# Unit order on TensorE in the first batch of a fused attention and two-layer kernel, and the engine of some weight additions

## The chip, the cores and the metric

The kernel runs on one core of one Trainium2 chip. The metric is the device time of one execution in microseconds (us), the median of several runs. The engines are PE (TensorE), DVE (VectorE), ACT (ScalarE), POOL (GpSimd) and SP (SyncE, which here only issues DMAs).

## The reference

For 8 batches of 8 heads, 576 tokens and 64 features, a memory attention with 32 memory slots gives `x`; two feed-forward layers follow on the 4608 tokens of width 512:

```python
a = softmax(phi, over tokens)                  # 8 x 8 x 576 x 32
k_m, v_m = a^T k, a^T v                        # 8 x 8 x 32 x 64
x = softmax(q k_m^T / sqrt(64)) v_m            # -> 4608 x 512
x = (silu(x @ w_gate) * (x @ w_val)) @ w_out   # 512 -> 1536 -> 512
out = elu(x @ w_in) @ w_out2                   # 512 -> 2048 -> 512
```

The weights come as 64-bit floats. The kernel's matmuls run on pairs of 32-bit tiles, a high part and a low part, three matmuls for each product.

## The kernel before

**Weights.** `load_w` (L86) loads 128x512 doubles as pairs of 32-bit words (tile `wr`, 4 buffers) and turns them into fp32. For each piece ACT scales the upper words into `wv` (L100), DVE does four passes of 128x512 (L101 and L104, one tensor input; L102 and L105, two), and one or two last additions go to GpSimd. A gate piece (`load_wg`, tile `wg`) has one, L111. A split piece (`load_wo` for the first layer's output weights, `load_w2` for the second layer) is also rounded by ACT (L107) and has two, L108 and L109, that give `wlo`. `wv` and its partner `wc` have two buffers each, so the third piece waits until the first has had its last addition.

**First layer, first pass.** Heads are never brought back into token order for the gate. Instead `vw(b, p)` (L133) multiplies the value memory `vt` of batch b with gate piece p (8 matmuls `pvw`), and ACT (L143) and DVE (L144) split the result into high and low `vw`; `VW(b, 0)` serves units 0 and 1, `VW(b, 1)` units 2 and 3. The softmax weights `at` take the place of `x`. A unit u of a half batch (288 tokens) is `gate1` (six matmuls `pg`, then ACT tanh and DVE L176 make `s`) and `val1` (six matmuls `pv`, DVE L183 makes `h`, ACT L162 and DVE L164 split it to `hh` and `hl`). The four units of a half batch are followed, one half batch later, by `down1` (`pd`, 48 matmuls a half batch). `pg`, `pv`, `pd` and `pvw` share the three buffers of PSUM pool `ps_gv`.

**Attention.** `front_tasks(b)` transposes phi (`ps_aT`), multiplies it with k and v (`ps_kvm`, scaled by DVE L258 to `kvm`), and transposes the result (`ps_kvT`, copied to `kT` and `vt`). `back_tasks(b)` makes the scores (`ps_sc`, 8 matmuls for each half batch) and their softmax on DVE and ACT, up to `at` (L307, L308).

**Order.** The code before the batch loop does batch 0's attention, `vw(0, 0)`, four gate pieces for p = 1, and `vw(0, 1)` (L370). In the loop over b, `tick()` (L421) puts the tasks of the coming batches (`todo`) between the units of batch b; `done[0] + 3` over `spread` says how far it has come. For b = 0 `todo` starts with the four output weights alternating with batch 1's front. Tile's scheduler then orders each engine's queue; `issue_after` keeps what it covers behind a given instruction. Each engine runs its queue in order. The last gate and output pieces of this layer (p = 4 and 5, u = 4 to 11) are converted from batch 6 on; units 4 to 11 run in a second pass afterwards, and then the second layer.

Of the kernel before, what the change touches and what calls it, by code (L numbers as in the profile page):

```python
# [8 lines left out]
F32 = mybir.dt.float32  # L9
# [4 lines left out]
ALU = mybir.AluOpType  # L14
# [12 lines left out]
UA = 4  # L27
# [10 lines left out]
def attention_moe_moe(ctx: ExitStack, tc: tile.TileContext, qT, phiT, kv, kv4, w1g, w1o, w2, out):  # L38
    nc = tc.nc
    act = nc.scalar.activation  # L40
    tt = nc.vector.tensor_tensor
    stt = nc.vector.scalar_tensor_tensor
    mm = nc.tensor.matmul
    w1g, w1o, w2 = w1g.bitcast(I32), w1o.bitcast(I32), w2.bitcast(I32)
# [30 lines left out]
    last = {}  # L75
# [3 lines left out]
    def together(calls):  # L79
        first = calls[0]()  # L80
        with tc.issue_after(first.ins), tc.high_priority():
            for call in calls[1:]:
                call()


    def load_w(store, u, i, src, pool, split=True):  # L86
        raw = wr_p.tile([128, 512, 2], I32, tag="wr", name="wr")
        nc.sync.dma_start(out=raw, in_=src.rearrange("p (n t) -> p n t", t=2))
        lo32, hi32 = raw[:, :, 0], raw[:, :, 1]
        if split:  # L90
            hi = pool.tile([128, 512], F32R, tag="w", name="whi")
            lo = pool.tile([128, 512], F32R, tag="w", name="wlo")
        else:
            full = pool.tile([128, 512], F32, tag="w", name="wg")
        v = wt_p.tile([128, 512], F32, tag="wv", name="wv")
        c = wt_p.tile([128, 512], I32, tag="wc", name="wc")
        vi, cf = v.bitcast(I32), c.bitcast(F32)
        with tc.issue_after(last["h"].ins) if "h" in last else nullcontext():

            act(out=v, in_=hi32.bitcast(F32), func=AF.Copy, scale=2.0 ** -112)  # L100
            nc.vector.tensor_scalar(out=c, in0=vi, scalar1=3, scalar2=None, op0=ALU.logical_shift_left)  # L101
            stt(out=vi, in0=vi, scalar=-2 ** 31, in1=c, op0=ALU.bitwise_and, op1=ALU.bitwise_or)  # L102

            nc.vector.tensor_scalar(out=c, in0=vi, scalar1=-2 ** 23, scalar2=None, op0=ALU.bitwise_and)  # L104
            stt(out=cf, in0=lo32.bitcast(U32), scalar=2.0 ** -52, in1=cf, op0=ALU.mult, op1=ALU.mult)  # L105
            if split:
                act(out=hi, in_=v, func=AF.Copy)  # L107
                nc.gpsimd.tensor_tensor(out=v, in0=v, in1=hi.bitcast(F32), op=ALU.subtract)  # L108
                nc.gpsimd.tensor_tensor(out=lo, in0=v, in1=cf, op=ALU.add)  # L109
            else:  # L110
                nc.gpsimd.tensor_tensor(out=full, in0=v, in1=cf, op=ALU.add)  # L111
        store[u][i] = (hi, lo) if split else full


# [1 line left out]
    WO = [[None] for _ in range(NU1)]  # L116
# [3 lines left out]
        load_w(WG, p, k, w1g[p, k], pool, False)  # L120

    def load_wo(u, pool):
        load_w(WO, u, 0, w1o[u], pool)

    def load_w2(u, i, pool):
        load_w(W2, u, i, w2[u, :, i * 1024:(i + 1) * 1024], pool)
# [6 lines left out]
    def vw(b, p, pools):  # L133
        t = VW[b, p] = vx_p.tile([128, 2, 2, 512], F32R, tag="vx", name="vw")
        ps = [pool.tile([128, 512], F32, tag=tag, name="pvw") for pool, tag in pools]

        def head(j, g):
            r, c = slice(64 * g, 64 * g + 64), slice(32 * j, 32 * j + 32)
            return mm(ps[g][c], lhsT=Bs[b].vt[r, j, :], rhs=WG[p][j][r], start=True, stop=True)  # L139

        together([lambda j=j, g=g: head(j, g) for j in reversed(range(KD)) for g in (1, 0)])
        for g in range(2):
            act(out=t[:, 0, g, :], in_=ps[g], func=AF.Copy)  # L143
            tt(out=t[:, 1, g, :], in0=ps[g], in1=t[:, 0, g, :].bitcast(F32), op=ALU.subtract)  # L144

    def up1(ps, w, c0, at, s0):
        cs, ss = slice(c0, c0 + 128), slice(s0, s0 + HS)
        for g in range(2):
            wh, wl = w[:, 0, g, cs], w[:, 1, g, cs]
            ah, al = at[:, 0, g, ss], at[:, 1, g, ss]  # L150
            mm(ps, lhsT=wh, rhs=ah, start=g == 0, stop=False)  # L151
            mm(ps, lhsT=wh, rhs=al, start=False, stop=False)  # L152
            mm(ps, lhsT=wl, rhs=ah, start=False, stop=g == 1)  # L153

    def down(ps, w, hs, ms, start, stop):
        mm(ps, lhsT=w[0][:, ms], rhs=hs[0], start=start, stop=False)  # L156
# [181 lines left out]
    G2 = [(ps_gv, "g")] * 2  # L338
# [28 lines left out]
    for k in range(KD):  # L367
        load_wg(1, k, wa_p)
    load(Bs[1])
    vw(0, 1, G2)  # L370

    def down1(b, hf, hs, m):
        ps = ps_gv.tile([128, HS], F32, tag="g", name="pd")
# [18 lines left out]
    for b in range(B):  # L392
        todo = []
        bk = list(back_tasks(b + 1)) if b + 1 < B else []
        fr = list(front_tasks(b + 2)) if b + 2 < B else []
        if b == 0:
            wo = [lambda u=u: load_wo(u, wa_p) for u in range(UA)]
            f1 = [lambda: (Bs[1].phi(), load_q(Bs[1]))] + list(front_tasks(1)) + [lambda: Bs[2].phi()]
            for i in range(max(len(wo), len(f1))):
                todo += wo[i:i + 1] + f1[i:i + 1]  # L400
        if 1 <= b <= 4:
            bk += [lambda k=k, p=2 + (b - 1) // 2: load_wg(p, k, wa_p) for k in (0, 1) if b % 2] + \
                [lambda k=k, p=2 + (b - 1) // 2: load_wg(p, k, wa_p) for k in (2, 3) if b % 2 == 0]
        if b == B - 2:
            wb_p = ctx.enter_context(tc.tile_pool(name="wb", bufs=NWB))
            ps_vw = ctx.enter_context(tc.tile_pool(name="ps_vw", bufs=1, space=PSUM))
            V2 = [(ps_vw, "vw"), (ps_gv, "g")]
            fr += [lambda u=u: load_wo(u, wb_p) for u in (4, 5, 6)]
        if b == B - 1:
            fr.append(lambda: load2(0))  # L410
            fr += wg_tasks(4) + [lambda: load_wo(7, wb_p), lambda: vw(0, 2, V2), lambda: load_wo(8, wb_p)]
            fr += wg_tasks(5) + [lambda: load_wo(9, wb_p), lambda: vw(0, 3, V2), lambda: load_wo(10, wb_p),
                                 lambda: load_wo(11, wb_p)]
        for i in range(max(len(bk), len(fr))):
            todo += fr[i:i + 1] + bk[i:i + 1]
        if b + 1 < B:
            todo += vw_tasks(b + 1)
        done = [0, 0]
        spread = 18 if b == 0 else 16 if b < B - 2 else 24

        def tick():  # L421
            done[0] += 1
            upto = min(len(todo), -(-len(todo) * (done[0] + 3) // spread))
            while done[1] < upto:
                todo[done[1]]()
                done[1] += 1

        silu = b == B - 1
        tick()
        for hf in range(2):  # L430
            hs = []
            for u in range(UA):
                s = gate1(b, u, Bs[b].at, HS * hf, silu)
                tick()
                hs.append(val1(b, u, Bs[b].at, HS * hf, s, silu))
                tick()
                if prev:
                    down1(*prev, u)
                    tick()
            prev = b, hf, hs  # L440
        while done[1] < len(todo):
            tick()
        if b == B - 3:
            st_fr.close()
            st_ps.close()
# [179 lines left out]
```

## Time and profile before

| | |
|---|---|
| median of 3 runs | 1608.3 us (1608.15 to 1608.68) |
| profiled execution, its own time | 1609.4 us |
| its span | 1607.6 us |
| PE busy | 1533.4 us (95%) |
| DVE busy | 988.0 us (61%) |
| ACT busy | 654.0 us (41%) |
| POOL busy | 166.2 us (10%) |

The span runs from the first to the last instruction; 1.8 us of the profiled execution lie outside it. PE is busy almost everywhere but in the first 80 us, around 320 to 360 us, and around 800 to 900 us. Shares over the whole span hide this; the views below are read by stretch.

### The profile page before, as it was taken

To read this page: it belongs to the slowest core of one execution; us is meant where nothing else is said; L and a number is where in the kernel's file an instruction comes from. 1 tells how busy PE (TensorE), PEld (TensorE's weight loads), DVE (VectorE), ACT (ScalarE), POOL (GpSimd) and SP (SyncE) were. 2 spreads that over 40 slices of the span, in tenths; PEclk is the share of its full clock that TensorE was granted. 3 is DMA by queue.
4 is the path that set the end of the run, shared out by engine and by line. 5 is a ranking of instruction groups with operands and counts; after the bars stand their busy time and mean duration, and the time that the engine had idled before them with its cause. 6 is when DMAs were issued, how large, how long until landed. Compare 5 with 4: busy or idle time off the path is not lost.

```text
span 1607.6 us, 24193 instructions
## 1 busy us (share of the span) xinstructions
PE 1533.4 (95%) x9816; PEld 1311.5 (82%) x9816; DVE 988.0 (61%) x1702; ACT 654.0 (41%) x1249; POOL 166.2 (10%) x119
## 2 busy tenths in 40 slices
PE   3599999979999999999998999999999999999998
PEld 2478789769999999999976788888888888888887
DVE  7997876795444454435889755555555555555554
ACT  3455444543333333333544433334343434343333
POOL 1400010241101011000435100000000000000000
PEclk7799999999999999999999999999999999999999
DMA  8887332452322232211522101001010101010000
GB/s 346 293 307 265 109 112 75 170 192 72 106 77 82 73 102 86 73 60 45 157 85 74 53 1 45 9 6 48 1 53 0 53 0 53 1 53 1 27 1 27
DMA packets 62961, 136.32 MB, mean 85 GB/s; under 512 B 6528, under 2 KB 37248, under 8 KB 60800
## 3 DMA queue, kind: packets, MB, share of 16 engines
q1 hardware_dynamic: 53632, 125.32, 22.7%
q10 hardware_dynamic: 9216, 9.44, 1.7%
q8 instruction: 77, 1.26, 0.3%
q14 instruction: 36, 0.29, 0.1%
HBM read 96.99 MB, written 37.75 MB: 84 GB/s over the span
## 4 chain that ended last, share of the span: by engine, by line
PE 81%; DVE 14%; DMA 2%; issue 2%; ACT 1%; SPq 0%; POOL 0%; ACTq 0%; DVEq 0%; POOLq 0%
PE acc L565 7%; PE acc L564 7%; PE acc L566 7%; PE pu L538 7%; PE pu L539 7%; PE pu L540 7%; PE acc L156 4%; PE acc L157 4%; PE acc L158 4%; PE pg L151 3%; PE pv L151 3%; PE pv L153 3%; PE pg L153 3%; PE pv L152 3%; PE pg L152 3%; PE pvw L139 3%
## 5 line engine op out<-in xcount | busy, mean ns | idle before, releaser
L538 PE MATMUL pu<-x1s,whi 128*128 128x512 f32 x576 | 224.7, 390 | 2.5 <-DVE g L554 2.5
L564 PE MATMUL acc<-whi,hh 128*128 128x512 f32 x576 | 224.5, 390 | 2.1 <-ACT hh L162 2.1
L566 PE MATMUL acc<-whi,hl 128*128 128x512 f32 x576 | 222.4, 390 | 3.3 <-DVE hl L164 3.3
L540 PE MATMUL pu<-x1s,wlo 128*128 128x512 f32 x576 | 224.8, 390 | 0.0
L539 PE MATMUL pu<-x1s,whi 128*128 128x512 f32 x576 | 224.7, 390 | 0.0
L565 PE MATMUL acc<-wlo,hh 128*128 128x512 f32 x576 | 224.2, 389 | 0.0
L553 DVE SCALAR_TENSOR_TENSOR g<-e,g 128x512 f32<-128x512 f32 x144 | 107.5, 747 | 157.5 <-ACT g L552 157.5
L162 ACT ACTIVATE hh<-g 128x512 fp32r<-128x512 f32 x144 | 91.0, 632 | 216.9 <-DVE g L554 216.9
L551 ACT ACTIVATE e<-g 128x512 f32<-128x512 f32 x144 | 90.8, 631 | 210.0 <-DVE g L550 210.0
L183 DVE SCALAR_TENSOR_TENSOR h<-s,pv 128x288 f32<-128x288 f32 x192 | 86.5, 451 | 140.8 <-PE pv L153 118.6
L164 DVE TENSOR_TENSOR hl<-g,hh 128x512 fp32r<-128x512 f32 x144 | 99.9, 694 | 88.3 <-ACT hh L162 88.2
L156 PE MATMUL acc<-hh,whi 128*128 128x288 f32 x512 | 151.0, 296 | 0.0
L157 PE MATMUL acc<-hh,wlo 128*128 128x288 f32 x512 | 150.6, 294 | 0.0
L158 PE MATMUL acc<-hl,whi 128*128 128x288 f32 x512 | 149.4, 295 | 0.0
L162 ACT ACTIVATE hh<-h 128x288 fp32r<-128x288 f32 x192 | 85.1, 443 | 138.9 <-DVE h L183 137.2
L164 DVE TENSOR_TENSOR hl<-h,hh 128x288 fp32r<-128x288 f32 x192 | 97.0, 505 | 63.0 <-ACT hh L162 62.8
L550 DVE TENSOR_SCALAR g<-pu 128x512 f32<-128x512 f32 x144 | 99.1, 689 | 55.2 <-PE pu L540 51.8
L566 PEld LDWEIGHTS acc<-whi,hl 128*128 128x128 f32 x576 | 108.0, 188 | 28.4 <-DVE hl L164 6.1
L151 PE MATMUL pg<-at,vw 128*128 128x288 f32 x384 | 119.4, 311 | 10.4 <-DVE vw L144 6.0
L564 PEld LDWEIGHTS acc<-whi,hh 128*128 128x128 f32 x576 | 108.3, 188 | 25.4 <-ACT hh L162 3.0
L538 PEld LDWEIGHTS pu<-x1s,whi 128*128 128x128 f32 x576 | 108.3, 188 | 25.3 <-DVE g L554 2.9
L539 PEld LDWEIGHTS pu<-x1s,whi 128*128 128x128 f32 x576 | 108.5, 188 | 22.6
(87 smaller groups left out, 3187.9 us busy)
## 6 DMA issues: line engine op xcount, KB each, us to landing
kvr<-kv SPq DMA_DIRECT2D x32, 512.0 KB, 7.9
wr<-w SPq DMA_DIRECT2D x32, 512.0 KB, 3.6
wr<-w1g SPq DMA_DIRECT2D x24, 512.0 KB, 4.9
qr<-qT SPq DMA_DIRECT2D x16, 576.0 KB, 5.9
atd<-at SPq DMA_DIRECT2D x8, 1152.0 KB, 5.3
p1d<-p ACTq DMA_DIRECT2D x64, 144.0 KB, 2.0
p1l<-p1d SPq DMA_DIRECT2D x16, 576.0 KB, 4.1
at<-atd SPq DMA_DIRECT2D x8, 1152.0 KB, 5.2
```

The source lines that it names most:

```text
L151: mm(ps, lhsT=wh, rhs=ah, start=g == 0, stop=False)
L156: mm(ps, lhsT=w[0][:, ms], rhs=hs[0], start=start, stop=False)
L157: mm(ps, lhsT=w[1][:, ms], rhs=hs[0], start=False, stop=False)
L158: mm(ps, lhsT=w[0][:, ms], rhs=hs[1], start=False, stop=stop)
L162: act(out=hh, in_=h, func=AF.Copy)
L164: tt(out=hl, in0=h, in1=hh.bitcast(F32), op=ALU.subtract)
L538: mm(ps, lhsT=wh[:, k, :], rhs=xh, start=k == 0, stop=False)
L539: mm(ps, lhsT=wh[:, k, :], rhs=xl, start=False, stop=False)
L540: mm(ps, lhsT=wl[:, k, :], rhs=xh, start=False, stop=k == KD - 1)
L564: mm(accs[c], lhsT=hs[0][:, cs], rhs=wh, start=u == 0, stop=False)
L565: mm(accs[c], lhsT=hs[0][:, cs], rhs=wl_, start=False, stop=False)
L566: mm(accs[c], lhsT=hs[1][:, cs], rhs=wh, start=False, stop=u == NU2 - 1)
```

## The change

Three things are changed. `vw(0, 1)` is called after unit 1 of the first half batch, no longer ahead of the loop. For b = 0 `tick` starts four steps later (`- 1` for `+ 3`), and each task that it issues is put behind the last matmul that `up1` had issued by then. The last additions of all 24 gate pieces and of output pieces 0 to 3 go to DVE.

```diff
-    def load_w(store, u, i, src, pool, split=True):
+    def load_w(store, u, i, src, pool, split=True, own=False):
...
-                nc.gpsimd.tensor_tensor(out=v, in0=v, in1=hi.bitcast(F32), op=ALU.subtract)
-                nc.gpsimd.tensor_tensor(out=lo, in0=v, in1=cf, op=ALU.add)
+                part = tt if own else nc.gpsimd.tensor_tensor
+                part(out=v, in0=v, in1=hi.bitcast(F32), op=ALU.subtract)
+                part(out=lo, in0=v, in1=cf, op=ALU.add)
             else:
-                nc.gpsimd.tensor_tensor(out=full, in0=v, in1=cf, op=ALU.add)
+                tt(out=full, in0=v, in1=cf, op=ALU.add)
...
-        load_w(WO, u, 0, w1o[u], pool)
+        load_w(WO, u, 0, w1o[u], pool, own=u < UA)
...
-            mm(ps, lhsT=wl, rhs=ah, start=False, stop=g == 1)
+            last["pe"] = mm(ps, lhsT=wl, rhs=ah, start=False, stop=g == 1)
...
-    vw(0, 1, G2)
...
-            upto = min(len(todo), -(-len(todo) * (done[0] + 3) // spread))
+            upto = min(len(todo), -(-len(todo) * (done[0] + (3 if b else -1)) // spread))
             while done[1] < upto:
-                todo[done[1]]()
+                with nullcontext() if b else tc.issue_after(last["pe"].ins):
+                    todo[done[1]]()
                 done[1] += 1
...
+                if (b, hf, u) == (0, 0, 1):
+                    vw(0, 1, G2)
```

The changed file has one line more ahead of L108, so what was L139 is L140 in the rows of the change. This is PE's queue before, from `vw(0, 0)` to the first matmuls of batch 0's first unit; `ps_aT`, `ps_kvm`, `ps_kvT` and `ps_sc` are batch 1's attention, but the last `ps_aT` row, which is batch 2's:

```order
L139 MATMUL pvw<-wg,vt 32x512 x8
L235 MATMUL ps_aT<-ident,ph 128x128 x8
L229 MATMUL ps_aT<-ident,ph 128x128
L251 MATMUL ps_kvm<-kvr,a 32x128 x40
L265 MATMUL ps_kvT<-ident,kvm 128x128 x2
L280 MATMUL ps_sc<-qr,kT 32x288 x8
L235 MATMUL ps_aT<-ident,ph 128x128 x4
L139 MATMUL pvw<-wg,vt 32x512 x8
L151 MATMUL pg<-at,vw 128x288
```

And this is PE's queue in the change, from behind unit 1's `pg` to the first matmul of unit 2 (18 matmuls, `pg` and `pv` of unit 0 and `pg` of unit 1, stand between `vw(0, 0)` and the first row):

```order
L236 MATMUL ps_aT<-ident,ph 128x128 x4
L152 MATMUL pv<-at,vw 128x288
L153 MATMUL pv<-at,vw 128x288
L154 MATMUL pv<-at,vw 128x288
L152 MATMUL pv<-at,vw 128x288
L153 MATMUL pv<-at,vw 128x288
L154 MATMUL pv<-at,vw 128x288
L236 MATMUL ps_aT<-ident,ph 128x128 x4
L140 MATMUL pvw<-wg,vt 32x512 x8
L152 MATMUL pg<-at,vw 128x288
```

Units 0 and 1 of batch 0 now stand ahead of `vw(0, 1)`; of batch 1's front only the first eight transposes do. Its `ps_kvm` comes behind units 2 and 3, its `ps_kvT` and scores behind the first rows of `pd`.

DVE's queue before, in the conversions of the four gate pieces of p = 1:

```order
L101 TENSOR_SCALAR wc<-wv 128x512
L102 SCALAR_TENSOR_TENSOR wv<-wv,wc 128x512
L104 TENSOR_SCALAR wc<-wv 128x512
L105 SCALAR_TENSOR_TENSOR wc<-wr,wc 128x512
L101 TENSOR_SCALAR wc<-wv 128x512
L102 SCALAR_TENSOR_TENSOR wv<-wv,wc 128x512
L212 TENSOR_REDUCE nmx<-ph 128x2
L258 TENSOR_SCALAR kvm<-ps_kvm,rs 128x2x64 x2
```

The same place in the change:

```order
L105 SCALAR_TENSOR_TENSOR wc<-wr,wc 128x512
L184 SCALAR_TENSOR_TENSOR h<-s,pv 128x288
L105 SCALAR_TENSOR_TENSOR wc<-wr,wc 128x512
L177 SCALAR_TENSOR_TENSOR s<-s,pg 128x288
L112 TENSOR_TENSOR wg<-wv,wc 128x512
L165 TENSOR_TENSOR hl<-h,hh 128x288
L112 TENSOR_TENSOR wg<-wv,wc 128x512
L184 SCALAR_TENSOR_TENSOR h<-s,pv 128x288
```

The additions L112 stand in DVE's queue, and `s`, `h` and `hl` of units 0 and 1 among the conversions; `nmx` of batch 2 and `kvm` of batch 1 have moved behind all conversions of p = 1.

## Rows read from the trace of the kernel before

**Rows 1.** The page, part 1: busy time, share of the span, instructions.
```profile
PE 1533.4 (95%) x9816; PEld 1311.5 (82%) x9816; DVE 988.0 (61%) x1702; ACT 654.0 (41%) x1249; POOL 166.2 (10%) x119
```
**Rows 2.** Stretches of 40 us: length, busy us and instructions, PE clock, DMA share, GB/s.
```profile
0.00:40.00 40.00, 15.74 (x172) 7.87 (x176) 28.64 (x51) 15.13 (x29) 6.42 (x11) 0.73 0.89 347
40.00:80.00 40.00, 23.81 (x276) 16.66 (x269) 39.73 (x65) 17.39 (x38) 17.00 (x12) 0.76 0.80 290
...
400.00:440.00 40.00, 40.00 (x325) 37.00 (x324) 19.41 (x42) 15.22 (x33) 6.32 (x4) 1.00 0.35 119
```
**Rows 3.** Three chosen stretches, same columns (PE, PEld, DVE, ACT, POOL).
```profile
12.70:80.20 67.50, 35.27 (x402) 21.68 (x402) 66.88 (x112) 27.94 (x60) 22.79 (x16) 0.70 0.84 317
80.20:160.00 79.80, 77.89 (x912) 63.97 (x918) 69.77 (x153) 45.40 (x107) 2.56 (x2) 1.00 0.80 287
312.90:361.10 48.20, 39.21 (x304) 33.74 (x303) 46.57 (x71) 23.98 (x51) 21.25 (x15) 0.99 0.62 207
```
**Rows 4.** PE's waits from 28 to 100 us: total us, times, longest.
```profile
PE ps_kvT L265 <- DVE kvm L258: 7.1, 1, 7.1
PE ps_aT L235 <- ACT ph L215: 6.8, 3, 5.2
```
**Rows 5.** PE in order of time: start us, busy us, idle before and releaser.
```profile
50.07 0.69 PE L265 MATMUL ps_kvT<-ident,kvm 128*128 128x128 f32 x2 [7.06 <-DVE kvm L258]
...
55.50 0.61 PE L151 MATMUL pg<-at,vw 128*128 128x288 f32 x1
...
68.96 0.44 PE L153 MATMUL pg<-at,vw 128*128 128x288 f32 x1
69.20 0.44 PE L151 MATMUL pg<-at,vw 128*128 128x288 f32 x1
...
75.10 0.29 PE L151 MATMUL pg<-at,vw 128*128 128x288 f32 x1
75.23 0.29 PE L152 MATMUL pg<-at,vw 128*128 128x288 f32 x1
...
77.03 0.72 PE L280 MATMUL ps_sc<-qr,kT 64*32 64x288 f32 x16 [0.37 <-ACT kT L268]
...
80.73 0.30 PE L153 MATMUL pv<-at,vw 128*128 128x288 f32 x1
...
361.24 0.61 PE L151 MATMUL pg<-at,vw 128*128 128x288 f32 x1 [3.47 <-DVE vw L144]
```
**Rows 6.** DVE groups, 12.7 to 80.2 us: busy us, mean ns, idle before.
```profile
L102 DVE SCALAR_TENSOR_TENSOR wv<-wv,wc 128x512 int32<-128x512 int32 x12 | 11.9, 994 | 0.2
...
L164 DVE TENSOR_TENSOR hl<-h,hh 128x288 fp32r<-128x288 f32 x2 | 2.8, 1416 | 0.0
```
**Rows 7.** The same groups of DVE from 80.2 to 160 us.
```profile
L164 DVE TENSOR_TENSOR hl<-h,hh 128x288 fp32r<-128x288 f32 x16 | 7.2, 448 | 1.5 <-ACT hh L162 1.5
...
L102 DVE SCALAR_TENSOR_TENSOR wv<-wv,wc 128x512 int32<-128x512 int32 x3 | 2.0, 683 | 0.0
```
**Rows 8.** DVE in order of time, the last gate conversions of p = 1 and after.
```profile
50.27 0.41 DVE L101 TENSOR_SCALAR wc<-wv 128x512 int32<-128x512 int32 x1
50.61 0.68 DVE L105 SCALAR_TENSOR_TENSOR wc<-wr,wc 128x512 f32<-128x512 uint32 x1
51.21 0.68 DVE L102 SCALAR_TENSOR_TENSOR wv<-wv,wc 128x512 int32<-128x512 int32 x1
...
59.89 0.68 DVE L144 TENSOR_TENSOR vw<-pvw,vw 128x512 fp32r<-128x512 f32 x1
```
**Rows 9.** POOL in order of time, last gate addition of p = 1.
```profile
51.37 1.68 POOL L111 TENSOR_TENSOR wg<-wv,wc 128x512 f32<-128x512 f32 x1 [3.68 <-DVE wc L105]
```
**Rows 10.** The chain that ended last: start us, us, what; a batch's `ps_kvm`.
```profile
109.30 2.38 PE ps_kvm L251 x80
```
**Rows 11.** PE's waits from 280 to 400 us.
```profile
PE pg L151 <- DVE vw L144: 5.7, 2, 3.5
```
**Rows 12.** DMA issues up to 160 us: count, KB each, median us to landing.
```profile
ph<-phiT SPq DMA_DIRECT2D x8, 576.0 KB, 4.5
```

## Prediction

> **What bounds the kernel now.** I read the page first, then the span in stretches, then in each weak stretch PE's waits and the engine that they name. PE is busy 1533.4 us of the 1607.6 [rows 1], so no more than 74 us can be won without taking matmuls away, and the change takes none. The stretches say where these lie: PE is idle 24.3 us in the first 40 and 16.2 in the next 40, and not at all from 400 to 440 [rows 2]. From 12.7 to 80.2 us it is DVE that is full (66.9 of 67.5 us), with PE at 35.3 and a mean granted clock of 0.70; from 80.2 to 160 PE is full (77.9 of 79.8) and DVE has 10 us to spare; from 312.9 to 361.1 DVE is full again (46.6 of 48.2) and PE idles 9.0 [rows 3]. So the start is bound by DVE, then PE takes over, and around 340 DVE bounds once more.
>
> What PE waits for in the start is batch 1's attention: 7.1 us for `kvm` and 6.8 us for phi's softmax [rows 4]. Both stand in PE's queue ahead of batch 0's first unit, and `kvm` stands in DVE's queue among the conversions. The gap before `ps_kvT` at 50.07 is one piece of 7.06 us [rows 5]. After such a gap PE runs at the lower of its two levels (1.2 GHz): its 288-column matmuls start 0.24 us apart at 68.96, and 0.13 us apart at 75.10, at 2.4 GHz [rows 5].
>
> **The change: the additions.** Up to 80.2 us POOL does 16 additions, 22.8 us of its time [rows 3]. They cost DVE something too. L102 takes 994 ns in the mean of twelve there and 683 where POOL has next to nothing to do; L164 takes 1416 against 448 [rows 6, 7]. Read in this way, L102 and L164 lose 3.7 and 1.9 us; L101, L104, L105, L218, L289 and L298 lose 7.6 us more between them. Together that is 13.2 us, or 0.83 us for each addition on POOL. On DVE an addition is a pass with two tensor inputs like L105 or L102, which start 0.60 us apart at 50.61 and 51.21 [rows 8]; I take 0.61. So in the start DVE pays 16 x 0.61 = 9.8 and gets 13.2 back: 3.4 us.
>
> The Trainium skill (SBUF — State Buffer, Who interferes with whom) says that a DVE instruction with two SBUF inputs and a GpSimd instruction that reads SBUF exclude each other for a whole instruction, whichever starts first. The rows agree that there is a loss, at 0.83 us against the 1.42 us that a POOL addition lasts; with the whole 1.42 the start would give 22.8 - 9.8 = 13.0 us in place of 3.4.
>
> **The order.** Now when the pieces come. *Gate pieces of p = 1.* Before, DVE ends the last pass at 51.2 and POOL adds until 53.05 [rows 8, 9]. In the change the same point on DVE has 8 additions more (4.9 us) and six instructions of units 0 and 1 (`s`, `h`, `hl` at some 0.4 each, 2.3 us), less `nmx`, two `kvm` and an L101 that moved behind it (2.1 us), less what POOL took from DVE by then (eight additions at 0.83, 6.6 us): 51.2 + 4.9 + 2.3 - 2.1 - 6.6 = 49.7, some 3.4 us earlier. *`VW(0, 1)`.* From there thirteen DVE rows follow up to the second L144, nine of 0.60 and four of 0.34 us [rows 8]: 6.8 us, so 56.5, against 60.5 before (59.89 + 0.6). *Output pieces 0 to 3.* Another 10 us of such rows, with four of units: 66.5, against 80.1 before, because the scores of batches 1 and 2 no longer stand between them.
>
> PE starts batch 0's units at about 35, when `at` and `vw(0, 0)` are there, not at 55.5 [rows 5]. Units 0 and 1 and eight transposes at the lower clock last until 42; then PE waits for the gate pieces until 49.7, does `vw(0, 1)`, waits again until 56.5, and has units 2 and 3, batch 1's `ps_kvm` and unit 4 done at about 65.5. Before, PE has the same five units done at 80.9 [rows 5], and beside them batch 2's `ps_kvm` (2.4 us [rows 10]), three scores (0.7 each [rows 5]), ten transposes and two `ps_kvT` (some 1.9 together): 6.4 us of matmuls that the change still owes. So PE stands at 65.5 + 6.4 = 72 where it stood at 80.9: **9 us ahead**. From there it has the 96 matmuls of `down1` of batch 0 (12.8 us at 0.13) and three units, so it need not run dry before batch 1's `at`, which by the same count of rows comes at 79 and 85.
>
> Can that be kept? DVE is only 3.4 us ahead, and PE 9. In 80.2 to 160 us DVE has 10 us to spare [rows 3], so most of PE's lead can be followed. Against it: the batch of attention that stood ready before is not there, and PE takes its inputs in order. SP's queue has changed as well: batch 0's `at` store and the four output pieces go ahead of phi of batch 2, which can be fetched only when batch 1's ninth transpose is through (about 58), and lands 4.5 us later [rows 12], at 62.5; DVE wants it at about 63, with everything of the units queued behind. A slip there stops DVE for a microsecond. Between 3.4 (DVE's own gain) and 9 I take **7 us**.
>
> *The second DVE-bound stretch.* From 312.9 to 361.1 POOL has 15 additions, of which eight are gate pieces that move to DVE. They give back 8 x 0.83 = 6.6 us and cost 8 x 0.61 = 4.9: 1.7 us for DVE. PE waits there on DVE's `vw` (5.7 us in two waits [rows 11]) and the longer, 3.47 us, is followed by 18 matmuls at 0.24 us [rows 5], 2 us lost to the clock. If the gap shrinks enough, that returns too. Bounds: nothing, where output pieces on POOL still hold DVE, to 6 us; I take **2.5 us**. The eight gate pieces of p = 2 and 3, up to 240 us, fall where DVE has slack: nothing. From 400 us on PE is full [rows 2] and its queue hardly differs.
>
> Sum: 1609.4 - 7 - 2.5 = 1599.9 for an execution like the profiled one. The median is 1.1 us below that one, so **1598.8 us**.
>
> **Rivals.** *The additions alone count* (chance 0.14): PE's lead is eaten as it takes batch 1's and 2's attention in order behind DVE, and only DVE's 3.4 and 1.7 us remain: 1603.2. For it speaks that DVE is the full engine in both stretches; against it that PE's longest waits are for order, not for DVE's total. *The lead is lost altogether* (0.11): DVE halts for phi's landing, each halt leaves PE a gap, and each gap brings some 2 us at the lower clock; two or three such gaps and the 7 us are gone: 1607. *Slower* (0.10): before, batch 2's scores were done by 85 us, a batch ahead; without that reserve PE waits for `s`, `vw` or scores in each of batches 1 to 6. A wait of 1.5 us and the slower clock behind it, 3 us a batch, is 18 us against the 9.5 gained: 1617. It decides if the mean loss per batch exceeds 1.6 us. Against it stands DVE's slack of 10 us in 80. *The full lock* (0.05): each addition gives back 1.42 us, 13.0 us in the start and 11.4 - 4.9 = 6.5 later, 1588.8; the skill's page named above states that rule, the group means speak against it. That the change does not do what it says is out: the queues show both parts.
>
> **How the numbers follow.** The forecast of 1598.8 has 0.60, with 1593 to 1603 as its own range. About 0.2% (3.2 us) is what a measurement of this kernel can tell from no change. Faster by more than that, below 1605.1: 0.60 + 0.13 + 0.05, so 0.78; within it 0.13; slower 0.09. For eight in ten the range takes in the full lock and most of the case of a lost lead: 1589 to 1607.
>
> **What would show it.** In the profile of the change: no DVE row of L102 or L164 above 0.75 us before 80 us and no POOL addition before 280; the first `pg` before 37 us; the gate pieces of p = 1 done by 50 and `VW(0, 1)` by 57; batch 0's unit 4 by 66; PE idle from 28 to 81 us down from 23 to some 15 us, and two gaps of 4 to 7 us in place of the one before `ps_kvT`. From 80 to 280 PE's idle time should be no more than 3 us above before. The 48 us of the late stretch should shrink by 2 to 3. I am wrong if DVE shows idle time before 66 us (a DMA or ACT holds it), if PE's queue stops for `kvm` or `at` of batch 1, or if PE's waits grow in every batch up to 280 us.

## Result, and the profile after the change

| kernel | median of its runs, us | ratio to before, 95% interval |
|---|---|---|
| before | 1608.49 (1608.15 to 1611.86) | |
| changed | 1592.23 (1591.82 to 1594.32) | 0.9897 (0.988 to 0.9914) |

The change makes the kernel faster by 1.0%: 16.3 us between the medians, 17.6 between the two profiled executions (1609.4 and 1591.8 us). The forecast was 1598.8, a gain of 9.5, with a range from 1589 to 1607. So the sign and the range hold, and the gain was sized at somewhat more than half of what it is.

The page of the changed kernel, part 1 (busy time, share of the span, instructions), answers to [rows 1]:

```profile
PE 1526.8 (96%) x9816; PEld 1307.7 (82%) x9816; DVE 977.2 (61%) x1734; ACT 653.7 (41%) x1249; POOL 121.5 (8%) x87
```

The span went from 1607.6 to 1590.0 us. PE does the same 9816 matmuls; it is idle for 63.2 us in place of 74.2, which is 11.0 us, and busy for 6.6 us less. The second number is easily passed over: fewer busy microseconds for the same matmuls mean that PE spent less time at the lower of its two levels (the mean granted clock of the two executions is 0.981 before and 0.986 now).

The same stretches as in [rows 2, 3] (length, busy us and instructions of PE, PEld, DVE, ACT, POOL, then PE's clock, DMA share, GB/s):

```profile
0.00:40.00 40.00, 17.64 (x166) 11.32 (x167) 29.09 (x60) 15.13 (x30) 0.76 (x7) 0.74 0.92 363
40.00:80.00 40.00, 29.25 (x335) 22.73 (x338) 38.16 (x81) 21.30 (x47) 0.00 (x0) 0.79 0.74 249
...
80.20:160.00 79.80, 75.89 (x913) 59.45 (x904) 75.31 (x164) 44.22 (x104) 0.00 (x0) 1.00 0.89 315
312.90:361.10 48.20, 44.42 (x318) 38.22 (x317) 41.67 (x75) 25.29 (x54) 14.15 (x10) 0.93 0.52 176
```

PE does 5.4 us more in 40 to 80 us. The last row covers the same time as before and not the same work, which now stands 12 us earlier. The steps that took 48.2 us before take 42.8 now:

```profile
300.60:343.40 42.80, 39.70 (x310) 34.43 (x308) 39.49 (x76) 24.08 (x50) 7.68 (x6) 1.00 0.66 222
```

DVE has become a little less full there (92%, before 97%), and POOL does 6 additions beside it in place of 15. PE's waits from 28 to 81 us, total us, times and longest, answer to [rows 4]:

```profile
PE pvw L140 <- DVE wg L112: 12.3, 2, 7.3
PE pg L152 <- ACT at L308: 3.2, 1, 3.2
PE pg L152 <- ACT vw L144: 1.7, 1, 1.7
PE pg L154 <- DVE vw L145: 1.6, 1, 1.6
```

The waits for `kvm` and phi are gone from this stretch; PE waits for the gate pieces, as the order makes it. In order of time (start us, busy us, idle before and releaser) these are the first `pg`, `VW(0, 1)` and the end of unit 4:

```profile
32.79 0.61 PE L152 MATMUL pg<-at,vw 128*128 128x288 f32 x1 [3.20 <-ACT at L308]
...
48.11 1.11 PE L140 MATMUL pvw<-wg,vt 64*32 64x512 f32 x8 [7.30 <-DVE wg L112]
...
64.31 0.29 PE L154 MATMUL pv<-at,vw 128*128 128x288 f32 x1
```

And the DVE groups of 12.7 to 80.2 us (busy us, mean ns, idle before), which answer to [rows 6]:

```profile
L102 DVE SCALAR_TENSOR_TENSOR wv<-wv,wc 128x512 int32<-128x512 int32 x12 | 8.1, 684 | 0.1
...
L112 DVE TENSOR_TENSOR wg<-wv,wc 128x512 f32<-128x512 f32 x8 | 5.3, 677 | 0.0
...
L165 DVE TENSOR_TENSOR hl<-h,hh 128x288 fp32r<-128x288 f32 x7 | 3.1, 450 | 0.5 <-ACT hh L163 0.4
```

With POOL silent, L102 is at 684 ns (994 before) and L165 at 450 (1416).

**How far PE is ahead.** The tool for the rest is the lead: how much earlier than before a kernel starts the same step. Steps that both kernels have are the first matmuls of `VW(b, p)`, read from PE's rows in order of time. Behind 395 us the leads no longer move within the first layer. All numbers are us, from the profiled execution of each kernel; what was run is told below.

| kernel | VW(1, 0) | VW(3, 0) | VW(5, 0) | VW(7, 0) | behind 395 us |
|---|---|---|---|---|---|
| changed | 10.8 | 13.0 | 11.6 | 12.3 | 17.6 |
| order alone | 4.4 | -0.6 | -6.0 | -6.7 | -5.7 |
| additions alone | 5.9 | -2.6 | 0.4 | 0.2 | 6.3 |
| gate p = 0, 1 back on POOL | 3.6 | 1.5 | -1.4 | -0.6 | 4.3 |
| output 0 to 3 back on POOL | 8.4 | 6.4 | -0.4 | -0.7 | 4.4 |
| gate p = 2, 3 back on POOL | 10.3 | 12.2 | 3.7 | 3.0 | 10.2 |
| gate p = 4, 5 back on POOL | 9.8 | 11.1 | 9.8 | 10.5 | 11.0 |
| idle additions beside | 2.0 | 2.6 | -1.6 | -0.9 | 3.7 |
| only VW(0, 1) moved | -0.8 | -2.9 | 0.8 | -0.8 | 4.5 |
| order alone, PE filled | 4.2 | 3.8 | 0.2 | 0.3 | 0.9 |

The start gives 12.3 us, and the late stretch 5.3. Two limits go with these leads. Four of the kernels have the same queues on PE and DVE up to 260 us: the changed one, the one with gate p = 4, 5 given back, and the two told below that have all output additions, or all additions, on DVE. At VW(6, 0) their leads are 12.4, 10.5, 11.2 and 11.7, so a lead is good to some 2 us, and the 12.3 is from the highest of the four. And some profiled executions lie off their kernel's median: gate p = 0, 1 given back with 1605.4 us (median 1600.1), idle additions with 1605.7 (1602.3), all additions on DVE with 1577.0 (1581.4). The leads are read for where something is lost, the ratios below for how much. Up to batch 4 the columns are not quite the same amount of work, since the changed kernel owes some attention there. When every matmul is counted at its spacing at 2.4 GHz, the changed kernel has done at 71.4 us what before had done at 81.0: 9.6 us ahead.

### The profile page after: what moved, and what is told of

The parts are those of the page before. It is cut to its first block, busy times and chain, and to the rows that moved or that the text cites. A ratio compares the mean times of both kernels' runs of the same rounds, so it can differ in the third digit from the quotient of the medians.

```text
span 1590.0 us, 24178 instructions
## 1 busy us (share of the span) xinstructions
PE 1526.8 (96%) x9816; PEld 1307.7 (82%) x9816; DVE 977.2 (61%) x1734; ACT 653.7 (41%) x1249; POOL 121.5 (8%) x87
## 4 chain that ended last, share of the span: by engine, by line
PE 82%; DVE 13%; DMA 2%; issue 2%; ACT 1%; SPq 0%; ACTq 0%; DVEq 0%
PE acc L568 8%; PE acc L567 8%; PE acc L569 8%; PE pu L541 7%; PE pu L542 7%; PE pu L543 7%; PE acc L157 4%; PE acc L158 4%; PE acc L159 4%; PE pg L152 3%; PE pv L152 3%; PE pv L154 3%; PE pg L154 3%; PE pv L153 3%; PE pg L153 3%; PE pvw L140 2%
## 5 line engine op out<-in xcount | busy, mean ns | idle before, releaser
L165 DVE TENSOR_TENSOR hl<-g,hh 128x512 fp32r<-128x512 f32 x144 | 99.9, 694 | 87.7 <-ACT hh L163 87.6
L165 DVE TENSOR_TENSOR hl<-h,hh 128x288 fp32r<-128x288 f32 x192 | 89.4, 466 | 62.1 <-ACT hh L163 62.1
```

Source lines behind the costliest of these rows:

```text
L165: tt(out=hl, in0=h, in1=hh.bitcast(F32), op=ALU.subtract)
```

## The experiments

All were run with the kernel before beside them (medians 1609.7 to 1610.8 us), so ratios are compared; a difference in us is a difference of ratios times 1609 (by that count the change gives 16.6). One thing limits most of them: the scheduler orders the queues anew for every edit. Only the run with the idle additions has the queues of PE, DVE and ACT row by row as in the changed kernel, and the four kernels named above are alike up to 260 us. With the other edits some 40 to 180 of DVE's first 440 rows stand elsewhere, so each sizes its edit together with the order that came of it.

**The order alone, and the additions alone.** For the first, in the changed kernel:

```diff
-                tt(out=full, in0=v, in1=cf, op=ALU.add)
+                nc.gpsimd.tensor_tensor(out=full, in0=v, in1=cf, op=ALU.add)
...
-        load_w(WO, u, 0, w1o[u], pool, own=u < UA)
+        load_w(WO, u, 0, w1o[u], pool)
```

> The changed kernel with every addition of load_w given back to GpSimd: the order alone. Known: before 1608.5 us, changed 1592.2. Theory 1 (the parts add up): of the 12.3 us that PE leads by at batch 1 some 9 are the order's and 3.4 the additions', and the late stretch gives its 5 to the additions: 1608.5 - 9 = 1599.5 us, the first vw of batch 1 starting at about 78.5 us (75.7 in the changed kernel, 86.5 before). Theory 2 (the order carries the whole start): 1608.5 - 12.3 = 1596, vw of batch 1 by 76 to 77. Theory 3 (PE takes its inputs in order, so the order is worth little as long as DVE is slow): 1605 or more, vw of batch 1 after 83.

Measured: 1614.2 us, ratio 1.0024 (1.0014 to 1.0034). The order alone is slower than before, by 3.9 us. The third theory's bound (1605 or more) takes the time in, but no theory had a loss, and VW(1, 0) came at 82.1, ahead of the third's 83. The second is the kernel before with the lines of `load_w` and `load_wo` from the change, and its order as it was:

> The kernel before with the gate's additions and those of output pieces 0 to 3 on VectorE: the additions alone. Theory 1 (the parts add up): 3.4 us at the start and some 5 in the late stretch, 1608.5 - 8.4 = 1600 us, vw of batch 1 at 83. Theory 2 (only the late stretch is the additions'): 1603.5, vw of batch 1 at 86. Theory 3 (the additions carry the start, the order little): 1608.5 - 10 - 5 = 1594 to 1596, vw of batch 1 at 77 or before. As the prediction's rival had it: 1608.5 - 3.4 - 1.7 = 1603.4.

Measured: 1602.0 us, 0.9951 (0.9939 to 0.9963), 7.9 us faster. The total is the first theory's, but not its parts: the lead of 5.9 us at VW(1, 0) is gone at VW(3, 0), and 6 us come in the late stretch. So alone the two parts give +3.9 and -7.9, and together -16.6: most of the gain belongs to neither, it is there only with both. Where does the additions' early lead go? DVE and PE of that kernel in order of time:

```profile
79.84 0.56 DVE L259 TENSOR_SCALAR kvm<-ps_kvm,rs 128x128 f32<-128x128 f32 x2
81.86 1.35 DVE L213 TENSOR_REDUCE nmx<-ph 128x2 f32<-128x1152 f32 x1 [1.46 <-DMA ph<-phiT]
```
```profile
85.38 0.63 PE L140 MATMUL pvw<-wg,vt 64*32 64x512 f32 x4 [3.34 <-DVE s L177]
```

and its clock, in stretches:

```profile
80.00:86.00 6.00, 2.66 (x32) 1.23 (x34) 4.54 (x10) 3.52 (x10) 0.00 (x0) 1.00 1.02 387
86.00:92.80 6.80, 6.80 (x50) 4.09 (x36) 6.75 (x18) 2.62 (x5) 0.00 (x0) 0.50 0.89 358
```

DVE is early and finds phi not landed, with the DMA engines full (share 1.02 by the row); `s` is queued behind, PE stands for 3.34 us, and then runs 6.8 us at the lower clock. Up to 250 us DVE waits for phi 6.1 us in four waits; in the changed kernel it is 3.1 and before 2.5. The order alone loses in another place:

```profile
PE ps_kvT L266 <- DVE kvm L259: 2.9, 2, 1.5
```
```profile
115.30:129.00 13.70, 13.14 (x96) 7.32 (x99) 11.39 (x23) 5.93 (x12) 3.00 (x2) 0.50 0.87 308
```

PE's waits there are short (two for `kvm`, 2.9 us in all, from 80 to 240 us), but three stretches between 91 and 174 us, 23.9 us together, run at a clock of 0.50. At half the speed that is some 12 us lost, and the changed kernel has 1.00 from 60.2 to 240 (two of the kernels that share its queues there have one stretch of 3.4 us, at 106).

**Pieces given back one group at a time.** In the changed kernel, with `u` the number of the gate pair:

```diff
-                tt(out=full, in0=v, in1=cf, op=ALU.add)
+                (nc.gpsimd.tensor_tensor if u < 2 else tt)(out=full, in0=v, in1=cf, op=ALU.add)
```

and with `u in (2, 3)` or `u >= 4` for the other gate pairs; for output pieces 0 to 3, `own=u < UA` is left out.

> The changed kernel with the additions of the gate pieces p = 0 and 1 given back to GpSimd (8 of the 16 at the start), those of output pieces 0 to 3 on VectorE: the counterpart of the run with the output pieces given back (12 us slower). Theory 1 (each delay of VectorE at the start comes back enlarged, as PE runs into short waits up to 240 us and into the lower clock behind them): PE's VW(0, 1) starts 2 to 4 us later than at 48.1, the lead is down by 8 to 13 us at batch 5, 1592 + 10 = 1602. Rival (the parts add up; 22 us for all, less 6 for the late pieces, less 12 for the output pieces): 1592 + 4 = 1596.

> The changed kernel with the additions of output pieces 0 to 3 given back to GpSimd (8 of the 16 at the start, from 50 to 66 us); the gate's stay on VectorE. With all given back the changed order was 22 us slower than the changed kernel, 6 of which are the late stretch's. Theory 1 (each addition at the start counts alike): half of 16 us, so 1592 + 8 = 1600. Rival (the gate pieces of p = 1 decide, PE waits for them 10.3 us with GpSimd against 7.3): 1592 + 2. Rival (the output pieces decide, since down1 of the first half waits for them and PE's clock falls): 1592 + 13.

> The changed kernel with the additions of the gate pieces p = 2 and 3 given back to GpSimd (8 additions between 115 and 240 us). The prediction put them at nothing, since VectorE has slack there: 1592 within 1.5 us, the first vw of batches 1 and 2 at 75.7 and 101.4 as in the changed kernel. Rival (they stretch VectorE's rows just where PE has short waits for it, in 120 to 160 us VectorE is busy 38.8 of 40): 3 to 6 us slower, with PE's waits between 120 and 240 us longer or a stretch at the lower clock there that the changed kernel has not.

> The changed kernel with the eight additions of the gate pieces p = 4 and 5 (the late stretch) given back to GpSimd, all else as changed: it sizes the late stretch. Theory 1 (those eight make the 5 us that the lead grows by between 290 and 380 us): 1592.2 + 5 = 1597 us, the lead over before constant at about 12.3 us from there on. As predicted (2.5 us, the rest comes from elsewhere): 1594.7. Rival (nothing: the seven output additions that stay on GpSimd hold VectorE anyway, and the gap closes because PE arrives earlier): 1592.2.

| given back to POOL | ratio | 95% interval | us slower than changed |
|---|---|---|---|
| gate p = 0, 1 | 0.9940 | 0.9924 to 0.9955 | 6.9 |
| output 0 to 3 | 0.9972 | 0.9961 to 0.9982 | 12.1 |
| gate p = 2, 3 | 0.9933 | 0.9921 to 0.9945 | 5.8 |
| gate p = 4, 5 | 0.9936 | 0.9922 to 0.9951 | 6.3 |

Each group of eight costs 6 to 12 us. They add up to 31 us, but all of them given back cost 20.4 (1.0024 against 0.9897): a lead can be lost once only. The third theory held for the output pieces; for the gate pieces p = 0 and 1 the interval lies between the two theories. The late pieces are 6.3 us, and their lead stays at 10.5 to 11.0 behind 250 us where the changed kernel's grows: here the first theory holds, not the prediction's 2.5.

The pieces p = 2 and 3, which the prediction put at nothing, have their own lesson. From VW(3, 0) to VW(4, 0) the lead falls from 12.2 to 2.8, in the changed kernel from 13.0 to 9.2. Between them stands this, on DVE:

```profile
156.26 0.76 DVE L299 TENSOR_TENSOR sc<-sc,smx 128x576 f32<-128x576 f32 x1
159.78 1.35 DVE L213 TENSOR_REDUCE nmx<-ph 128x2 f32<-128x1152 f32 x1 [2.76 <-DMA ph<-phiT]
161.05 0.60 DVE L259 TENSOR_SCALAR kvm<-ps_kvm,rs 128x128 f32<-128x128 f32 x2
```

`kvm` stands behind `nmx` here and ahead of it in the changed kernel, phi lands 2 us later, PE waits 2.9 us for `kvm`, and from 161.3 to 168.1 its clock is 0.50. POOL's two additions at 149 and 151 us stretch L105 from 0.64 to 0.97 us and L290 from 0.74 to 0.85 beside them: the additions' own price is below 0.5 us, and what comes of it in this execution is 5.6. The 5.8 us of the runs agrees; why phi lands later is not shown, and as `kvm` has changed places, the order that came of the edit is a part of the price.

**Of the order, the one moved step.** The changed kernel with `done[0] + 3` for every batch and without the hold behind the last matmul:

```diff
-            upto = min(len(todo), -(-len(todo) * (done[0] + (3 if b else -1)) // spread))
+            upto = min(len(todo), -(-len(todo) * (done[0] + 3) // spread))
...
-                with nullcontext() if b else tc.issue_after(last["pe"].ins):
-                    todo[done[1]]()
+                todo[done[1]]()
```

> The changed kernel without its two rules on the tasks of batch 0 (three ticks ahead as before, and not held behind the last value matmul): of the order only VW(0, 1) is still moved behind unit 1. Theory 1 (the attention of batches 1 and 2 then stands on VectorE and PE ahead of output pieces and units again, and half of the start's gain of order goes): 1592.2 + 4 to 5 = 1597 us. Rival (the one moved step lets units 0 and 1 run early, and that is all of it): 1592 to 1593. Rival (the rules do it all, the early units only fill what was idle): 1601, the first vw of batch 1 at 84.

Measured: 1603.2 us, 0.9956 (0.9942 to 0.997), 9.5 us slower than the changed kernel, and VW(1, 0) at 87.3. In time that is the last rival (0.9956 of 1608.5 is 1601.4; VW(1, 0) is 3 us later than it said): with the additions on DVE but without the two rules, nothing is left of the start's gain, and the time is that of the additions alone. So the rules are needed. Whether they would do it all without the moved step was not run.

**What POOL takes from DVE.** Does an addition on POOL cost by what waits for it, or by what it does to DVE? The changed kernel, with 16 additions on POOL that write a tile which nobody reads:

```diff
-                part(out=lo, in0=v, in1=cf, op=ALU.add)
+                part(out=lo, in0=v, in1=cf, op=ALU.add); own and [beside(hi, lo) for _ in range(2)]
...
-                tt(out=full, in0=v, in1=cf, op=ALU.add)
+                tt(out=full, in0=v, in1=cf, op=ALU.add); u < 2 and beside(full, full)
...
+    beside = lambda x, y: nc.gpsimd.tensor_tensor(out=idle_t, in0=x.bitcast(F32), in1=y.bitcast(F32), op=ALU.add)
```

> The changed kernel, and beside it GpSimd does 16 additions that nothing waits for: as many and as large as before, each reading a piece that VectorE has just finished (p = 0 and 1 of the gate, output pieces 0 to 3). It tells what GpSimd takes from VectorE apart from the wait for GpSimd's result. Theory 1 (the loss is in VectorE's instructions beside GpSimd's): 16 x 0.83 = 13 us more on VectorE before 80 us, L102 near 0.99 us there, the first vw of batch 1 10 us later (at 86) and most of the changed kernel's lead gone: 1592 + 10 or more = 1602 to 1606. Rival (the loss was the chain through GpSimd, 1.4 us behind each piece and two buffers held): VectorE's rows as in the changed kernel and the time within 2 us of it.

Measured: 1602.3 us, 0.9954 (0.994 to 0.9969): 9.2 us slower than the changed kernel, VW(1, 0) at 84.6. As nothing else in the queues differs and no engine waits for POOL, this is shown to be what POOL's additions do to DVE. The first theory holds in time, but the rows that pay are others. DVE's groups from 12.7 to 70 us, in the changed kernel and then with the idle additions:

```profile
L102 DVE SCALAR_TENSOR_TENSOR wv<-wv,wc 128x512 int32<-128x512 int32 x12 | 8.1, 684 | 0.1
...
L101 DVE TENSOR_SCALAR wc<-wv 128x512 int32<-128x512 int32 x12 | 5.0, 418 | 4.5 <-ACT wv L100 4.4
L104 DVE TENSOR_SCALAR wc<-wv 128x512 int32<-128x512 int32 x12 | 4.9, 417 | 0.1
```
```profile
L102 DVE SCALAR_TENSOR_TENSOR wv<-wv,wc 128x512 int32<-128x512 int32 x12 | 8.8, 742 | 0.1
...
L101 DVE TENSOR_SCALAR wc<-wv 128x512 int32<-128x512 int32 x12 | 8.4, 706 | 4.5 <-ACT wv L100 4.4
L104 DVE TENSOR_SCALAR wc<-wv 128x512 int32<-128x512 int32 x12 | 6.4, 543 | 0.1
```

An addition that starts when DVE ends a piece meets the next piece's L101 and L104, not L102. L101, L102, L104, L105 and L110 lose 7.5 us together up to 70 us, where POOL has not yet done all of its 16 additions. Counted row by row up to 80 us DVE loses 9.7 us, or 0.6 for each addition. In the order alone, where POOL adds where it did before, L102 is at 1185 ns and L165 at 1173 (up to 70 us):

```profile
L102 DVE SCALAR_TENSOR_TENSOR wv<-wv,wc 128x512 int32<-128x512 int32 x12 | 14.2, 1185 | 0.2
...
L165 DVE TENSOR_TENSOR hl<-h,hh 128x288 fp32r<-128x288 f32 x3 | 3.5, 1173 | 0.0
```

The same count of L101 to L105, L165 and L290 makes 12.9 us, or 0.81 for each of 16: the prediction's 0.83.

**The clock by itself.** The order alone, and twelve transposes that nobody reads behind the matmuls of `ps_kvm` in batches 2 and 3:

```diff
+            for _ in range(12 if self.b in (2, 3) else 0):
+                with tc.issue_after(last["pe"].ins): nc.tensor.transpose(out=fill, in_=ident, identity=ident)
```

> The order alone (1614 us, 22 above the changed kernel), and in batches 2 and 3 twelve transposes of the identity, which nobody reads, behind the matmuls of ps_kvm: 1.4 us of work each time, as long as PE's two waits for kvm that stand there just ahead of the stretches at the lower clock from 91.4 to 94.8 and from 115.3 to 129.0 us. Theory 1 (of what the order alone loses between 80 and 205 us, two thirds or more is the lower clock behind those waits, so work in their place costs nothing and keeps the clock): neither stretch is there, 1614 - 6 to - 8.5 = 1606 to 1608. Rival (it is the waits themselves and those behind them that cost): 1614 within 2. Rival (the transposes are only work more): 1614 + 2.8 = 1617.

Measured: 1610.1 us, 0.9994 (0.9985 to 1.0004), against 1.0024 (1.0014 to 1.0034) without them: PE was given 24 matmuls more and the kernel became 4.8 us faster. In the profiled executions the lead behind 395 us goes from -5.7 to 0.9. The stretches in order:

```profile
80.00:119.50 39.50, 35.90 (x459) 26.33 (x462) 37.31 (x78) 21.81 (x51) 3.41 (x2) 1.00 0.82 277
119.50:122.90 3.40, 3.40 (x30) 1.91 (x19) 3.40 (x8) 2.29 (x4) 0.00 (x0) 0.50 0.94 358
122.90:198.00 75.10, 73.61 (x866) 63.66 (x872) 63.64 (x140) 37.80 (x93) 2.54 (x2) 1.00 0.67 238
```

Of 23.9 us at 0.50 between 80 and 200 us 3.4 are left. So the direction is the first theory's and the size a little short of it, and some 5 of the 20 us between the order alone and the change go with PE's short waits and the clock behind them. That it is the clock alone is not shown, since PE's queue differs in more than the transposes: at 95 us the scores now stand ahead of a unit's `pg`, in the order alone behind it. How the rest divides is argued from the traces, not shown.

**All additions on DVE.** `own=True` for every output piece, and then `part = tt` for every piece, the second layer's too:

> The changed kernel with the additions of output pieces 4 to 11 on VectorE as well (16 additions between 160 and 360 us, the last ones beside PE's gaps of 0.9, 1.8 and 0.7 us and a stretch of 6.8 us at the lower clock around 343). Theory 1 (an addition on GpSimd takes more of VectorE than it costs there, 0.83 against 0.61 us, and delays what waits for it): the gaps and that stretch go, 3 to 6 us, a ratio to the changed kernel of 0.996 to 0.998. Rival (the late stretch is no longer bound by VectorE, whose share there is 33.5 of 40 us): no change. Rival (16 more passes, 9.8 us, in VectorE's queue ahead of the units): 2 to 4 us slower.

> The changed kernel with every addition of load_w on VectorE, the 64 of the second layer's pieces too. Theory 1 (as for the output pieces): these 64 give VectorE back some 64 x 0.2 = 14 us in the stretch from 720 to 880 us, where PE idles 7.5 us in gaps of 2.5 to 0.9; half of that goes, 4 us beside those of the output pieces. Rival (the 64 additions of 0.61 us, 39 us, stand in VectorE's queue between a unit's g and its hl, so the gaps before acc grow): 3 to 10 us slower than with the output pieces alone.

Measured: 1588.1 us, 0.9869 (0.9854 to 0.9883), and 1581.4 us, 0.983 (0.9815 to 0.9845). Both are the first theory in time, the second with more than it forecast; the stretch at the lower clock around 343 us is halved (3.4 us left) with the output pieces alone and gone with all. The second kernel beats both kernels of this case, by 1.7% and 0.7%. From 800 to 880 us, in the changed kernel and with all on DVE, and DVE's costliest group there from 780:

```profile
800.00:880.00 80.00, 71.38 (x302) 55.81 (x303) 77.74 (x107) 38.49 (x63) 40.59 (x26) 1.00 0.18 60
```
```profile
L556 DVE SCALAR_TENSOR_TENSOR g<-e,g 128x512 f32<-128x512 f32 x14 | 17.5, 1255 | 2.6 <-ACT g L555 2.6
```
```profile
800.00:880.00 80.00, 79.37 (x350) 65.40 (x349) 75.69 (x136) 43.75 (x71) 0.00 (x0) 1.00 0.17 60
```
```profile
L556 DVE SCALAR_TENSOR_TENSOR g<-e,g 128x512 f32<-128x512 f32 x18 | 12.5, 705 | 3.2 <-ACT g L555 3.2
```

DVE does 136 instructions where it did 107, in less time, and PE's idle time there falls from 8.6 us to 0.6. Part of that is the window, since the same steps come 6 to 15 us earlier: from 720 to 960 us PE's idle time falls from 9.2 us to 3.4.

**Filling PE's wait at the start.** The kernel with all additions on DVE, and 36 transposes ahead of VW(0, 1):

```diff
+        for _ in range(36 if (b, p) == (0, 1) else 0):
+            nc.tensor.transpose(out=ps[0][:, 0:128], in_=ident, identity=ident)
```

> The kernel with all additions on VectorE (0.983 of before, 1581 us), and 36 transposes of the identity ahead of VW(0, 1), where PE waits 6.9 us for the last gate piece, up to 48.1 us. Theory 1 (the start up to 55 us is bound by VectorE, and from there PE runs units 2 and 3 at the lower clock up to 60.9 only because it had waited): PE is at 2.4 GHz by 48, units 2 and 3 and batch 1's ps_kvm are done 2 to 3 us earlier, and that is kept, 1581.4 - 2.5 = 1579. Rival (the two waits of 1.7 us for vw that follow bring the clock down again): 1581 within 1. Rival (PE arrives earlier and waits for VectorE later): 1581 within 1, with the first vw of batch 1 at 74 and that of batch 5 at 219 as without.

Measured: 1582.9 us, 0.9824 (0.9809 to 0.9839) against 0.983: no difference. The transposes end at 44.2 us, VW(0, 1) still waits 3.93 us, and the clock, at 1.00 up to there, falls again:

```profile
40.12 4.09 PE L143 MATMUL pvw<-ident 128*128 128x128 f32 x36
48.14 1.75 PE L140 MATMUL pvw<-wg,vt 64*32 64x512 f32 x16 [3.93 <-DVE wg L112]
```
```profile
38.20:48.50 10.30, 6.37 (x60) 5.77 (x66) 10.10 (x22) 4.78 (x9) 0.00 (x0) 1.00 0.67 238
48.50:58.70 10.20, 7.74 (x55) 4.98 (x43) 10.17 (x22) 5.56 (x12) 0.00 (x0) 0.50 0.62 195
```

In time that fits the first rival, but not its reason: the clock is at 0.50 from 48.5 us on, behind what is left of the wait for `wg` and ahead of the first wait for `vw`, which ends at 51.06. The gate pieces are ready at 48.1 us with the transposes and without, so DVE sets the time there. PE's `ps_kvm` does come 2.6 us earlier (57.9 in place of 60.5), as the first theory had it, but the gain is not kept: VW(1, 0) starts at 77.1 us, and at 76.2 without the transposes. As the queues behind differ too, what takes it is open.

## Why the prediction came out as it did

**The dates at the start were right.** Forecast and found: first `pg` before 37 (32.8), gate pieces p = 1 by 49.7 (48.0, where L112 ends), the last `vw` of VW(0, 1) by 56.5 (55.1), output pieces 0 to 3 by 66.5 (65.0), unit 4 by 65.5 (64.6). PE's idle time from 28 to 81 us was to fall from 23 to some 15: it is 14.3. The lead was counted as 9 at before's 80.9 us; by equal work it is 9.6. No addition ran on POOL there. Of the other signs two missed: POOL's first addition came at 272 us, not behind 280, and the late stretch shrank by 5.3 us, not by 2 to 3. One reading was off: the matmuls at 68.96 us [rows 5] were not slow because of the gap that ended at 50.07, since the clock was at 1.00 from 56.2 to 66.4 us in between; the gap they follow is a later one.

**The discount failed.** From 9 the prediction took 7, since DVE was only 3.4 us ahead and phi might halt it. In fact the lead went up, to 12.3 (10.5 to 12.4 in the four executions named above). PE's idle time from 80 to 240 us is 7.7 us against 7.1 before, as was foreseen. What differs is a stretch at the lower clock that only the kernel before has; in order of time, its PE row ahead of that stretch, and the stretch:

```profile
197.84 0.40 PE L151 MATMUL pv<-at,vw 128*128 128x288 f32 x1 [1.49 <-DVE s L176]
```
```profile
199.50:206.40 6.90, 6.90 (x32) 5.04 (x29) 4.99 (x8) 3.18 (x7) 2.55 (x2) 0.51 0.52 161
```

By equal work the lead goes from 8.8 us ahead of this stretch to 11.6 behind it. For this pair of executions that closes the account: 9.6 us, 2.7 more by 300 us, which is about what this stretch gives, and 5.3 in the late stretch are the 17.6 us. Some of it may be luck: one trace of the kernel before is kept, 2.7 us is near the scatter of the leads, and whether its other executions have the stretch is not shown. For it speaks that three kernels whose lead is gone have one at the same place (from 200 to 207 us with the output pieces given back and with the idle additions, from 203.7 to 207.1 with gate p = 0, 1). The clock stood in the prediction only as a price of the change's own gaps; that the kernel before had such a stretch to lose was in the trace and was not looked for.

**The rival of a lost lead named a mechanism that is real, for other kernels.** DVE halting for phi, PE's gap behind it and the lower clock behind that is what the traces show where the additions alone lose their early lead, and the kernel with p = 2 and 3 given back a part of it. The changed kernel was spared it: its DVE waits for phi 3.1 us in all. The rival had a chance of 0.11. It said that the whole of the start would be lost, and the additions alone, which meet it, keep nothing of theirs; its 1607 us was for the changed kernel and did not come.

**The additions: the price was right, the worth was not.** 0.83 us taken from DVE for each addition on POOL is borne out (0.81 and, beside other rows, 0.6). A net gain of 3.4 us was drawn from it, as if the start were a sum of DVE's time. By the traces the additions up to 240 us are worth 17 us of lead in the new order (10.5 with the late ones given back, -6.7 with all); in the old order they are worth 0.2. The step that failed is the one that let PE's and DVE's gains stand apart: PE keeps its lead only where DVE is early as well, and a small delay grows: the output pieces given back cost 2.4 us of lead at VW(1, 0) and 12.0 at VW(5, 0).

**The middle pieces were not worth nothing.** The prediction named DVE's slack as their cover, 10 us of 80 before. In the changed kernel DVE is busy 75.3 of 79.8 us from 80.2 to 160: the change had used up the cover that hid them.

**The late stretch was mis-sized.** 2.5 us were forecast and 6 given as the upper bound; the lead grows by 5.3, and eight additions given back cost 6.3. DVE's occupancy alone (1.7 us) was the wrong measure: PE's gap of 3.47 us ahead of `pg` [rows 5] is gone, and from 280 to 400 us PE is idle for 5.6 us where it was for 12.6. One stretch at the lower clock stays there, at 343 us in place of 360.

**The full lock was dismissed for the wrong reason.** The Trainium skill (SBUF — State Buffer, Who interferes with whom) lets the second instruction wait for the whole of the first. The prediction held that the group means speak against it. Row by row the trace of the kernel before agrees with the rule. These are two of POOL's additions, and DVE's rows beside them:

```profile
46.32 1.37 POOL L111 TENSOR_TENSOR wg<-wv,wc 128x512 f32<-128x512 f32 x1 [1.81 <-DVE wc L105]
...
53.57 1.69 POOL L108 TENSOR_TENSOR wv<-wv,whi 128x512 f32<-128x512 f32 x1 [0.53 <-DVE rs L219]
```
```profile
46.61 1.63 DVE L102 SCALAR_TENSOR_TENSOR wv<-wv,wc 128x512 int32<-128x512 int32 x1
...
54.04 0.84 DVE L285 STREAM_TRANSPOSE sc<-ps_sc 128x288 f32<-128x288 f32 x2
54.92 0.75 DVE L288 TENSOR_REDUCE mx<-sc 128x18 f32<-128x576 f32 x1
```

L102 starts 0.29 us behind the addition and ends at 48.24, 0.55 us behind the addition's end at 47.69; by itself it takes 0.68. Up to 80.2 us 15 DVE rows are stretched so, and every one ends at most 0.62 us behind the end of an addition: 0.55 for L102 and L105, 0.28 for L101 and L104, 0.31 for L164. They lose the 13.2 us that the prediction counted. Rows that read PSUM (L258, L176, L285), the reduction L288 and the reciprocal L297 keep their own length beside an addition. So what failed in the rival is its price, not its rule: a DVE row loses only what is left of the addition when it starts, and POOL's 1.42 us became 0.83 on average, 0.6 with the idle additions. The rival's time of 1588.8 is nearer to the result than the forecast, but for another reason.

## What to carry to other kernels

Where two engines feed each other, do not price two edits one by one: here each alone gave +3.9 and -7.9 us and both gave -16.6, since an early PE needs an early DVE. Ask of a lead not only how large it is but what it will meet next (a load not landed, a pair of matmuls with a round trip between), and look for stretches at the lower clock in the kernel before, as they can be won as well as lost. An operation put on an idle GpSimd is not free for VectorE: look at the single VectorE rows beside it, as a mean hides that some stand still until it ends and others do not notice it. Where VectorE is full, try the operation on VectorE.

## What was not expected of the hardware

A short wait is followed by the lower clock in one place and not in another. Behind the wait of 1.49 us for `s` at 197.84 us, shown above, the kernel before runs for 6.9 us at 0.51. Its next wait of that kind is as long, stands behind the same steps of the next batch, and the clock stays; the row, and the stretch around it:

```profile
232.86 0.40 PE L151 MATMUL pv<-at,vw 128*128 128x288 f32 x1 [1.49 <-DVE s L176]
```
```profile
230.00:240.00 10.00, 7.65 (x64) 4.54 (x63) 9.53 (x19) 4.80 (x11) 2.57 (x2) 1.00 0.28 83
```

Executions of one kernel differ too: twelve of the filled order alone lie between 1604.9 us, at a mean clock of 0.983, and 1612.9, at 0.979. What decides it, these runs leave open.

VectorE instructions with one input in SBUF suffer beside GpSimd as well: L101, a `tensor_scalar`, went from 418 to 706 ns in the mean of twelve. The Trainium skill (SBUF — State Buffer, Who interferes with whom) says that `tensor_scalar` can take the shared port in a faster mode; the rows agree, as every L101 and L104 that starts while an idle addition runs ends 0.28 or 0.29 us behind it. A count of instructions with two inputs alone would have missed 5 of the 7.5 us there.
